# A decode block's backward pass: the chunk load and its staging buffer become a ring of two, and the next chunk is loaded half a chunk ahead

## The chip, the cores and the metric

The kernel runs on one core of one Trainium2 chip. The metric is the device time of one execution in microseconds (us), lower is better. Executions of one kernel in the same rounds mostly lie within half a per cent of their median (the widest set, `ring_slots61`, runs from 1462.4 to 1474.6 us). All runs quoted here are of the fast state. "Faster" is said of a difference of more than 2%.

## The reference, cut to what matters

The program computes one transformer block for a single token (forward) and the gradients of nine inputs (backward). The attention has 32 heads of width 192 over a cache of 8192 positions; K and V have 100 MB each, and their gradients as much again.

```python
def _fwd_reference(A_x, A_k_cache, A_v_cache, A_wq, A_wo, B_x, ..., c, w_mod):
    mod = (_silu(c) @ w_mod).reshape(c.shape[0], 6, 1, -1)     # w_mod: 640 x 3840
    ...
    h = _layernorm(x, axis=-1) * (1 + ca) + sa
    x = x + ga * _A_ref(h, A_k_cache, A_v_cache, A_wq, A_wo)   # wq: 640 x 6144
    h = _layernorm(x, axis=-1) * (1 + cb) + sb
    x = x + gb * _B_ref(h, B_w1, B_w2, B_w3, B_w4)
    return x

def reference(...):
    _out, _vjp = jax.vjp(_f, A_x, A_k_cache, A_v_cache, A_wq, A_wo, B_w3, B_w4, c, w_mod)
    return (_out, *_vjp(grad_out))
```

Two matrices matter here, wq and w_mod. For a matrix W with y = x W the backward pass needs two things: W times the gradient of y (so W is read again), and the outer product of x with the gradient of y (a matrix as large as W, which is written). The kernel does both for 768 columns at a time, a **chunk** of 960 KB: eight chunks of wq, five of w_mod.

## The kernel before

The backward stage is a loop over 64 steps (32 heads, two halves of the cache). Each step loads 1.5 MB of V, computes dP, dS, dV and dK, and stores 3 MB. Between its parts the loop calls `slot()` four times, which runs the next pieces of side work from one list: the wo transposes (`g_do`), dWo (`g_dwo`), and the chunks (`g_chunk`, five pieces for each half of a chunk).

```python
    def load_w(view3, lo, hi):                 # one load buffer ("w", bufs=1)
        w = wst.tile([P, ND, CW], BF16, name="w_st", tag="w", bufs=1)
        nc.sync.dma_start(out=w[:, :, 0 : hi - lo], in_=view3[:, :, lo:hi])
        return w
    # ... (cut)
    def next_w():
        if wseq:
            view, n = wseq.pop(0)
            cur["next"] = load_w(view, n * CW, (n + 1) * CW)
    # ... (cut)
    def g_chunk(b, v3, rows, dst, n, acc, lay):          # half b of chunk n
        lo = n * CW
        if b == 0:
            cur["w"] = cur.pop("next")
            cur["stg"] = bst.tile([P, ND, CW], BF16, name="stg")   # one staging buffer
        w = cur["w"][:, :, b * PW : (b + 1) * PW]
        stg = cur["stg"][:, :, b * PW : (b + 1) * PW]
        # ... (cut) piece 1: cast of the vector
        yield
        wT = bst.tile([P, 15 * P], BF16, name="wT", tag="wT")
        transposed(0, cols, ND, wT)            # piece 2: first use of the loaded chunk (TensorE)
        # ... (cut)
        yield
        transposed(8, cols, ND, wT)            # piece 3: last use of this half
        if b == 1:
            next_w()                           # the load of the next chunk
        # ... (cut)
        yield
        # ... (cut) piece 4: matrix times vector
        for i in range(3):
            V_.tensor_scalar(out=stg[:, i, :], in0=v_bc, scalar1=rows[:, i : i + 1], ...)
        yield
        V_.tensor_tensor(out=acc, in0=ps, in1=acc, op=ALU.add)     # piece 5
        for i in range(3, ND):
            V_.tensor_scalar(out=stg[:, i, :], in0=v_bc, scalar1=rows[:, i : i + 1], ...)
        if b == 1:
            nc.gpsimd.dma_start(out=dst[:, :, lo : lo + CW], in_=cur["stg"])
        yield
    # ... (cut) the order of the side work: after every fourth pair of heads a w_mod chunk
    for t in range(NT):
        # ... (cut)
        jobs.append((5, g_dq(t)))              # half of a wq chunk
        if t % 4 == 3 and late:
            jobs.append((10, g_wm(late.pop(0))))   # a w_mod chunk, at once behind it
    jobs.append((2, g_finish_x()))
    for n in late + list(range(GX)):           # two w_mod chunks, one behind the other
        jobs.append((10, g_wm(n)))
    # ... (cut) the end of a step
        if s + 4 < NS:
            v_l[s + 4] = load_v((s + 4) // 2, s % 2)     # 1536 KB, SyncE's queue
        if s + 2 < NS:
            er_l[s + 2] = load_er(s + 2)                 # 8 KB, SyncE's queue
```

In the timelines below TensorE and SyncE take their instructions in the order of the program text: while TensorE waited 9.18 us for a chunk (until 1013.75 us) it ran nothing else, and while SyncE waited for a store (`ring_first_piece`) the V and er loads behind it waited too. Loads are issued by SyncE, stores by GpSimd. **er** is the 8 KB of (unnormalised) attention weights that TensorE needs for the dV of one step (matmul `dv_ps`); in the views `KB` is a tile (in this stage mostly the output buffers of dV and dK), `stg` the staging buffer, `w_st` the load buffer, DVE is VectorE, POOL is GpSimd, and PEld are TensorE's weight loads.

## Time and profile before

| | kernel before |
|---|---|
| time, median | 1498.7 us |
| profiled span | 1495.2 us |
| moved over the span | 576 MB, 385 GB/s |
| TensorE's waits for chunk loads, from 650 us on | 35.7 us in 4 |

The page's first part has busy time, share of the span and number of instructions of each engine; its last part the transfers (source, issuing queue, count, size).

```profile
PE 1143.8 (77%) x12579; PEld 773.2 (52%) x12579; DVE 1121.6 (75%) x1391; ACT 891.5 (60%) x1966; POOL 106.7 (7%) x190
...
v_sb<-in_A_v_cache_dram SPq DMA_DIRECT2D x128, 1536.0 KB
w_st<-in_A_wq_dram SPq DMA_DIRECT2D x16, 960.0 KB
w_st<-in_w_mod_dram SPq DMA_DIRECT2D x8, 960.0 KB
```

No engine is full over the span, and the chunk loads share SyncE's queue with the V loads. The rows of the page that show the DMA engines as the bound, and the three holes in their rate, stand in the prediction.

### The profile page before, as it was taken

Reading aid. Unit: us, or ns where it says so; the run is one execution under the profiler, and the core shown is the slowest. Engines: PE = TensorE matmul, PEld = TensorE weight load, DVE = VectorE, ACT = ScalarE, POOL = GpSimd, SP = SyncE. Lnnn points to the kernel's source line nnn. Section 1 sums busy time; section 2 is a strip of 40 time slices with the busy share of each in tenths; the row PEclk is TensorE's granted clock in tenths of the full one; section 3 lists DMA queues with packets and bytes.
Section 4 is the critical chain, followed back from the end, with each engine's and each line's share of the span. In section 5 each row is a group of like instructions: output and inputs, shape, how many; then the busy total and the mean of one; then the engine's idle time right before and its main releaser. Section 6 shows DMA issues by size and latency. Waiting matters only on the chain.

```text
span 1495.2 us, 30163 instructions
## 1 busy us (share of the span) xinstructions
PE 1143.8 (77%) x12579; PEld 773.2 (52%) x12579; DVE 1121.6 (75%) x1391; ACT 891.5 (60%) x1966; POOL 106.7 (7%) x190
## 2 busy tenths in 40 slices
PE   3999999999899997777777667766777576676564
PEld 1677777767677776544444434434444343444332
DVE  5999999999999994566767677756676576776465
ACT  1776777776777765655655555545555455555354
POOL 0000000000000000011011011010110110111010
PEclk8999999999999998655656675555565556655555
DMA  9999999999999986499999999998999989999797
GB/s 377 414 407 419 418 410 395 412 398 402 393 406 395 417 318 260 153 406 420 396 423 419 410 422 399 415 396 312 411 411 415 395 314 392 425 420 397 287 416 317
DMA packets 76471, 576.12 MB, mean 385 GB/s; under 512 B 7310, under 2 KB 25054, under 8 KB 35374
## 3 DMA queue, kind: packets, MB, share of 16 engines
q1 hardware_dynamic: 52074, 347.75, 59.0%
q0 software_dynamic: 24240, 226.44, 35.9%
q8 instruction: 98, 1.61, 0.4%
q14 instruction: 39, 0.32, 0.1%
q10 hardware_dynamic: 20, 0.00, 0.0%
HBM read 347.74 MB, written 226.43 MB: 384 GB/s over the span
## 4 chain that ended last, share of the span: by engine, by line
issue 52%; DVE 19%; PE 12%; ACT 9%; POOL 6%; DMA 1%; POOLq 0%; SPq 0%; DVEq 0%; ACTq 0%
DVE prod L275 9%; ACT vs L333 6%; DVE vs L326 4%; DVE prod L280 3%; PE mp L340 3%; PE dot_ps L286 2%; POOL out_dram L938 2%; POOL out_dram L948 2%; DVE S_h L290 2%; PE mp L344 2%; PE q_ps L248 1%; PE op L348 1%; DMA KB<-in_A_k_cache_dram 1%; PE po L378 1%; POOL out_dram L796 1%
## 5 line engine op out<-in xcount | busy, mean ns | idle before, releaser
L707 ACT CAST KB<-dv_ps 128x768 bf16<-128x768 f32 x512 | 377.3, 813 | 167.5 <-PE dv_ps L706 152.9
L695 PE MATMUL dot_ps<-pq,ident_bf 128*128 128x256 bf16 x1536 | 327.9, 398 | 57.9 <-DVE pq L686 57.9
L333 ACT ACTIVATE vs<-v_sb,Ef 128x192 bf16<-128x192 bf16 x896 | 323.4, 443 | 0.0
L706 PE MATMUL dv_ps<-KB,er_b 1*128 1x192 bf16 x2048 | 179.2, 319 | 145.2 <-ACT KB L707 137.0
L695 PEld LDWEIGHTS <-ident_bf 128*128 128x128 bf16 x1536 | 203.4, 136 | 161.3 <-issue 90.0
L711 DVE TENSOR_TENSOR KB<-qs_bc,dS 128x3072 bf16<-128x3072 bf16 x128 | 223.8, 1749 | 37.4 <-DMA out_dram<-KB 37.3
L686 DVE TENSOR_TENSOR pq<-v_sb,KB 128x3072 bf16<-128x3072 bf16 x128 | 223.7, 1748 | 0.0
L275 DVE TENSOR_TENSOR prod<-KB,qs_bc 128x6144 bf16<-128x6144 bf16 x64 | 214.5, 3352 | 10.2 <-DMA KB<-in_A_k_cache_dram 5.5
L340 PE MATMUL mp<-vs,KB 128*128 128x193 bf16 x2048 | 198.5, 250 | 3.6 <-DVE vs L326 3.1
L583 ACT COPY wT<-wT_ps 128x1024 bf16<-128x1024 bf16 x84 | 81.0, 964 | 200.6 <-PE wT_ps L582 197.2
L706 PEld LDWEIGHTS <-er_b 1*128 1x128 bf16 x2048 | 66.0, 103 | 241.8 <-issue 231.9
L340 PEld LDWEIGHTS <-KB 128*128 128x128 bf16 x2048 | 178.1, 99 | 23.5 <-issue 5.8
L286 PE MATMUL dot_ps<-prod,ident_bf 128*128 128x512 bf16 x384 | 97.3, 391 | 46.6 <-DVE prod L280 46.6
L326 DVE TENSOR_TENSOR vs<-v_sb,E 128x1728 bf16<-128x1728 bf16 x128 | 131.9, 1051 | 0.6 <-ACT E L314 0.6
L280 DVE TENSOR_TENSOR prod<-prod 128x3072 bf16<-128x3072 bf16 x64 | 112.1, 1752 | 0.6
L290 DVE TENSOR_REDUCE dP<-dot_ps 128x32 f32<-128x512 f32 x64 | 44.1, 689 | 90.8 <-PE dot_ps L695 90.8
L344 PE MATMUL mp<-vs,KB 128*64 128x193 bf16 x2048 | 110.7, 251 | 0.0
L344 PEld LDWEIGHTS <-KB 128*64 128x64 bf16 x2048 | 82.8, 110 | 21.1 <-issue 21.1
L582 PE MATMUL wT_ps<-ident_bf,w_st 128*128 128x128 bf16 (+1 forms) x470 | 51.7, 293 | 44.0 <-DMA w_st<-in_w_mod_dram 33.5
L286 PEld LDWEIGHTS <-ident_bf 128*128 128x128 bf16 x384 | 36.0, 99 | 89.4 <-issue 60.5
L774 DVE CAST vrow<-bc_t 3x128 bf16<-3x128 f32 x26 | 7.2, 278 | 98.2 <-PE bc_t L772 98.2
L938 POOL DMA_DIRECT2D out_dram<-KB x64 | 36.4, 569 | 589.5 <-ACT KB L707 589.3
(222 smaller groups left out, 953.6 us busy)
## 6 DMA issues: line engine op xcount, KB each, us to landing
v_sb<-in_A_v_cache_dram SPq DMA_DIRECT2D x128, 1536.0 KB
out_dram<-KB POOLq DMA_DIRECT2D x128, 1536.0 KB, 13.1
KB<-in_A_k_cache_dram SPq DMA_DIRECT2D x64, 1536.0 KB
w_st<-in_A_wq_dram SPq DMA_DIRECT2D x16, 960.0 KB
wo_st<-in_A_wo_dram SPq DMA_DIRECT2D x32, 480.0 KB
out_dram<-stg POOLq DMA_DIRECT2D x14, 960.0 KB, 12.6
out_dram<-stg_o POOLq DMA_DIRECT2D x17, 480.0 KB, 13.6
w_st<-in_w_mod_dram SPq DMA_DIRECT2D x8, 960.0 KB
```

Source lines behind the costliest of these rows:

```text
L275: V_.tensor_tensor(out=prod, in0=src, in1=vec[:, None, :].to_broadcast([P, JH, DH]), op=ALU.mult)
L280: V_.tensor_tensor(out=prod[:, :, 0:w], in0=prod[:, :, 0:w], in1=prod[:, :, w : 2 * w], op=ALU.add)
L286: T_.matmul(ps, lhsT=ident_bf, rhs=prod[:, :, k : k + TS], start=(k == 0), stop=(k == w - TS))
L326: V_.tensor_tensor(out=vs[:, 0:n, 0:DH].rearrange("p j (a b) -> p j a b", b=4), in0=v[:, v0 : v0 + n, :].rearrange("p j (a b) -> p j a b", ...
L333: A_.activation(out=vs[:, k, 0:DH], in_=v[:, v0 + k, :], func=ACT.Copy, scale=Ef[:, j0 + k : j0 + k + 1])
L340: T_.matmul(mp[:, 0:MW], lhsT=kb[:, j0 + k, 0:P], rhs=vs[:, k, 0:MW], start=(q == 0 and k == 0), stop=(z and k == JQ - 1), skip_group_chec ...
L344: T_.matmul(mp[p0 : p0 + 64, MO : MO + MW], lhsT=kb[:, j0 + k, P:DH], rhs=vs[:, k, 0:MW], start=False, stop=(z and k >= JQ - 2), skip_grou ...
L686: V_.tensor_tensor(out=pq[:, q], in0=v_l[s][:, q * JQ : (q + 1) * JQ, :], in1=do_bc[:, None, (s // 2) * DH : (s // 2 + 1) * DH].to_broadca ...
L695: T_.matmul(ps[:, q * JQ : (q + 1) * JQ, :], lhsT=ident_bf, rhs=pq[:, q, :, k : k + TS], start=(k == 0), stop=(k == DH - TS), skip_group_c ...
L706: T_.matmul(ps[:, b, k * DH : (k + 1) * DH], lhsT=er[p0 : p0 + 1, 2 * m + k, :], rhs=doh[p0 : p0 + 1, :], start=True, stop=True)
L707: A_.copy(out=dV4[:, 2 * q : 2 * q + 2, m * PW : (m + 1) * PW], in_=ps[:, :, 0:PW])
L711: V_.tensor_tensor(out=dK[:, lo:hi, :].rearrange("p j (a b) -> p j a b", b=4), in0=qh.rearrange("p (a b) -> p a b", b=4)[:, None, :, :].to ...
```

## The change

The intent: with one load buffer the next chunk can't be loaded before the last transpose of the current one. The change lets the gradient overwrite the chunk in place (each half only after its transposes), so that the former staging buffer is free to take the next chunk, and issues that load in piece 5 of the first half instead of piece 3 of the second. No memory is added.

```diff
     def next_w():
         if wseq:
             view, n = wseq.pop(0)
-            cur["next"] = load_w(view, n * CW, (n + 1) * CW)
+            if cur.setdefault("n", 0) % 2 == 0:
+                w = wst.tile([P, ND, CW], BF16, name="w_st", tag="w", bufs=1)
+            else:
+                w = bst.tile([P, ND, CW], BF16, name="stg")
+            cur["n"] += 1
+            nc.sync.dma_start(out=w, in_=view[:, :, n * CW : (n + 1) * CW])
+            cur["next"] = w
 ...
             cur["w"] = cur.pop("next")
-            cur["stg"] = bst.tile([P, ND, CW], BF16, name="stg")
-        w = cur["w"][:, :, b * PW : (b + 1) * PW]
-        stg = cur["stg"][:, :, b * PW : (b + 1) * PW]
+        w = stg = cur["w"][:, :, b * PW : (b + 1) * PW]
 ...
         transposed(8, cols, ND, wT)
-        if b == 1:
-            next_w()
 ...
-        if b == 1:
-            nc.gpsimd.dma_start(out=dst[:, :, lo : lo + CW], in_=cur["stg"])
+        if b == 0:
+            next_w()
+        else:
+            nc.gpsimd.dma_start(out=dst[:, :, lo : lo + CW], in_=cur["w"])
```

## The prediction

> **What bounds the kernel now.** I read the page's slices first. The span has a forward stage (to about 560 us), a short middle, and a backward stage from about 640 us on. The change touches the backward stage only. There the TensorE is busy seven tenths of the time and the DMA engines nearly always:
>
> ```profile
> PE   3999999999899997777777667766777576676564
> DMA  9999999999999986499999999998999989999797
> GB/s 377 414 407 419 418 410 395 412 398 402 393 406 395 417 318 260 153 406 420 396 423 419 410 422 399 415 396 312 411 411 415 395 314 392 425 420 397 287 416 317
> ```
>
> The reader should see that the third row of the backward part is flat at 395 to 425 GB/s, except for slices 28, 33 and 38 (312, 314, 287), and the last one. So the backward stage is bound by data movement, with three holes in it. I then asked for the waits of the backward stage alone (from 650 us), and looked for one that could make such holes:
>
> ```profile
> POOL out_dram L938 <- ACT KB L707: 585.3, 61, 25.9
> DVE vrow L774 <- PE bc_t L772: 98.2, 22, 15.0
> DVE stg L790 <- DMA out_dram<-stg: 6.0, 1, 6.0
> PE wT_ps L582 <- DMA w_st<-in_w_mod_dram: 33.5, 3, 14.9
> PE wT_ps L582 <- DMA w_st<-in_A_wq_dram: 2.2, 1, 2.2
> ```
>
> The columns are total us, times, longest. The big first row is only the store queue waiting for the next result. The fourth row is the one: TensorE stands still three times for the load of a w_mod chunk, 33.5 us in all. The timelines of SyncE (which issues the loads) and of TensorE show how one hole comes about:
>
> ```profile
> 988.91 0.33 SPq L270 DMA_DIRECT2D v_sb<-in_A_v_cache_dram  x1
> 989.34 0.50 SPq L551 DMA_DIRECT2D er_b<-eT_d  x1
> 992.69 0.38 SPq L188 DMA_DIRECT2D w_st<-in_w_mod_dram  x1
> ...
> 1001.83 2.74 PE L695 MATMUL dot_ps<-pq,ident_bf 128*128 128x256 bf16 x12
> 1013.75 1.03 PE L582 MATMUL wT_ps<-ident_bf,w_st 128*128 128x128 bf16 x8 [9.18 <-DMA w_st<-in_w_mod_dram]
> ```
>
> The load is issued at 992.69, its consumer is reached at about 1004.6 (1013.75 less 9.18), its data are there at 1013.75. The lead is 11.9 us, the flight 21.1 us. The other two are alike: issued 1174.96, wanted 1186.7, there 1196.09 (9.39 us waited); issued 1369.28, wanted 1379.3, there 1394.21 (14.92 us waited). TensorE takes its instructions in order, so the main path (dP, dV, dK of each half head) stands too, and about 10 us later the DMA queues have run dry. The engine table by stretch prices this:
>
> ```profile
> 650.00:1010.00 360.00, 257.35 (x2071) 154.90 (x2069) 244.49 (x340) 199.21 (x281) 40.90 (x70) 0.60 1.01 410
> 1010.00:1050.00 40.00, 26.53 (x227) 16.33 (x228) 26.86 (x36) 21.43 (x30) 3.58 (x6) 0.59 0.83 320
> 1050.00:1170.00 120.00, 90.25 (x715) 52.75 (x712) 81.04 (x125) 68.13 (x97) 12.08 (x22) 0.60 1.01 414
> 1170.00:1220.00 50.00, 31.02 (x246) 18.07 (x243) 28.56 (x36) 23.65 (x33) 4.09 (x7) 0.53 0.85 327
> 1220.00:1380.00 160.00, 113.92 (x959) 68.97 (x956) 116.81 (x187) 86.94 (x121) 20.92 (x35) 0.61 1.00 408
> 1380.00:1430.00 50.00, 28.11 (x225) 16.41 (x225) 24.54 (x37) 20.67 (x29) 3.76 (x7) 0.50 0.79 312
> ```
>
> The last two columns are DMA share and GB/s. Undisturbed stretches run at 408 to 414, call it 412; the three disturbed ones at 320, 327 and 312.
>
> **What the Trainium skill says.** "DMA: Bandwidth & Descriptors", section "Where 436 GB/s comes from", puts the fabric ceiling at 435 GB/s; the trace agrees in that no 40th of the span passes 425 here, so the flat parts have little left. The same page, "Issuing engines are not separate DMA queues", says that transfers of all issuing engines interleave on the same 16 DMA engines: this is why a 960 KB load that alone would need 2.4 us at 412 GB/s (my estimate from its size) takes 21 us behind a V load and beside the stores. "Perfetto Trace Analysis", section "Per-engine timelines", says that a hardware-issued DMA's profiled window does not hold its data movement; so I take flights from issue to consumer (21.1 us), not from the 0.38 us of the issue. "Trainium Kernel Development and Optimization", "Best Practices", says to double-buffer so that DMA overlaps compute: the trace shows what one buffer costs, 33.5 us.
>
> **The change, part by part.** The kernel has 13 chunks in this stage (8 of wq, 5 of w_mod), each worked in two halves of five pieces of side work. There are 206 pieces over 236 slots, four slots to a step; steps are 13.3 us apart (stores at 1079.22 and 1172.31 us, seven steps), so a piece comes every 13.3 / (4 x 206/236) = 3.8 us.
>
> Removed: nothing in instructions or bytes. The 130 scalings of 0.31 us stay, as do 13 loads and 13 stores. The load tile and the staging tile are the same two tiles; they now take turns as load and, in place, as output. Memory is equal.
>
> Moved: the load goes from piece 3 of a chunk's second half to piece 5 of its first half. Where a w_mod chunk follows a wq chunk there are, between issue and use, one dWo piece, three do pieces, five dq pieces and two of the new chunk: 11 pieces x 3.8 = 42 us, against a flight of 21 us. So waits one and two (9.2 + 9.4 us) go away. Between the last two w_mod chunks lie only 5 + 2 pieces, 27 us by that pace. In the trace the place is just after the er load of 1353.93, so about 1355, and the use at 1379.3: 24 us, against a flight of 24.9 us before, which then had one more V load (1365.97) ahead of it. So wait three goes from 14.9 us to 0 to 4 us, and a wait that short leaves the DMA queues filled.
>
> Added: the load must wait for the store of the chunk before the current one to land. Stores land after 12.6 us in the median, at most 19.8. That store is issued five pieces (19 us) earlier or more, so SyncE seldom waits, and then for a few us in which the next V load has no free buffer anyway (V loads come 10 to 16 us apart). The in-place writes come two pieces after the transposes that read the same half, so no engine waits for them. The scaling's one wait for the single staging buffer (6.0 us) goes.
>
> Sum, by bytes not moved at 412 GB/s: 40 x (1 - 320/412) = 8.9 us; 50 x (1 - 327/412) = 10.3 us; 50 x (1 - 312/412) = 12.1 us: 31.3 us together. It agrees with the 33.5 us of TensorE waits, since little was made up afterwards. I take off 3 us for what remains of wait three or of new small waits: 28 us gained. 1498.4 - 28 = 1470 us.
>
> **The rivals.** (1) The transfer was hidden anyway: the DMA is the bound and a TensorE wait costs nothing. For: 10 us of each wait pass with queues still at 420 GB/s. Against: the holes afterwards (share 0.83, 0.85, 0.79) are as large as the waits. Time then 1490 to 1498. (2) A new wait takes the old one's place: SyncE takes its loads in order and may stand for a landing store, holding V and er loads back, or the earlier 960 KB delays the small er loads behind it (TensorE waited once 5.95 us for one, at 1251 us). Against: the store is 19 us old by then. It would give back 5 to 15 us: 1475 to 1485. (3) More is won than the holes: earlier loads free SyncE, and steps speed up. Against: the flat parts are at 408 to 414 GB/s, and the whole of 650 to 1460 us at 412 would save only 33 us. Best case about 1462.
>
> **Range and chances.** The middle is 1470, with rival 3's cap below and rival 2 above: 1460 to 1487. A gain of 2% needs 29.4 to 30 us, that is almost all of the 31.3; I give it 0.38. Within 2%: 0.59. Slower by 2%: 0.03, only if in-place use serialises what I think free.
>
> **What would show it.** In the changed profile TensorE's wait for w_mod should fall from 33.5 to under 6 us; each w_mod load should be issued over 22 us before its first transpose; the GB/s row should have no slice near 310 before the last; TensorE's busy time should not change. I am wrong if holes remain with another releaser (er loads, V loads, stores of a chunk), if SyncE shows waits of over 10 us for a chunk's store, or if the holes vanish while the flat level sinks under 405.

## The result

The changed kernel takes 1463.3 us (median of 4 runs, 1461.9 to 1464.2) against 1498.7 us (4 runs, 1495.2 to 1500.4). The ratio is 0.9763, 95% interval 0.9744 to 0.9783: faster. Ratios in this document are those on record, taken from fast runs of the same rounds; they are not quite the ratio of the medians quoted.

The page of the changed kernel, with the rows of busy time, DMA share and rate in 40 slices:

```profile
PE 1142.1 (78%) x12579; PEld 774.0 (53%) x12579; DVE 1121.8 (77%) x1391; ACT 891.4 (61%) x1966; POOL 106.5 (7%) x190
...
DMA  9999999999999998289999999999999999999997
GB/s 375 416 411 419 399 418 409 401 388 411 405 396 395 416 401 308 91 329 415 394 426 425 403 417 422 412 407 409 424 395 422 387 395 428 413 426 394 422 418 328
```

Busy times are those of before within 2 us. The three holes at slices 28, 33 and 38 are gone: from slice 19 to slice 39 nothing is below 387. The engine table by stretch, over the same microseconds as the disturbed stretches of before, has DMA share and GB/s in its last columns (before: 0.83 and 320, 0.85 and 327, 0.79 and 312):

```profile
1010.00:1050.00 40.00, 30.30 (x254) 18.82 (x252) 28.38 (x43) 23.14 (x32) 4.74 (x8) 0.63 1.01 421
1170.00:1220.00 50.00, 38.85 (x305) 23.15 (x305) 34.28 (x46) 29.24 (x41) 6.58 (x11) 0.53 0.99 404
1380.00:1430.00 50.00, 34.26 (x273) 19.39 (x272) 35.49 (x38) 26.80 (x37) 5.68 (x10) 0.60 1.01 418
```

In the waits of TensorE for a transfer from 640 us on, no chunk is left; one row remains, for the small er loads. (The rows have the releaser, total us, times, longest.)

```profile
PE dv_ps L706 <- DMA er_b<-eT_d: 9.2, 4, 4.3
```

The timelines of SyncE and TensorE show the load and the first use of the second w_mod chunk (lead 42.0 us) and of the last one (26.0 us); neither use waits:

```profile
962.48 0.46 SPq L735 DMA_DIRECT2D stg<-in_w_mod_dram  x1
...
1004.44 1.06 PE L582 MATMUL wT_ps<-ident_bf,stg 128*128 128x128 bf16 x8
...
1335.36 0.51 SPq L735 DMA_DIRECT2D w_st<-in_w_mod_dram  x1
...
1361.40 1.03 PE L582 MATMUL wT_ps<-ident_bf,w_st 128*128 128x128 bf16 x8
```

**Where the time came from.** The 64 steps each issue one dV store, so the stores of the two traces can be laid side by side as a clock. The changed kernel is 0.1 us behind at step 28 and 9.3 us ahead at step 29; 8.2 ahead at step 41 and 17.8 at step 42; 17.2 at step 45 and 22.3 at step 46; 19.0 at step 55 and 33.3 at step 56; 34.1 at the last. The four jumps are 9.4, 9.6, 5.1 and 14.3 us. TensorE's waits of before at these places are 9.18, 9.39, 5.95 (for an er load, at 1251 us) and 14.92 us. Between the jumps the two kernels drift by up to some 5 us (the changed one is 4.8 us behind at step 19 and level again at step 21).

### The profile page after: what moved, and what is told of

Its sections match the earlier page's. It is cut to its first block, busy times and chain, and to the rows that moved or that the text cites. A ratio compares the mean times of both kernels' runs of the same rounds, so it can differ in the third digit from the quotient of the medians.

```text
span 1461.0 us, 30156 instructions
## 1 busy us (share of the span) xinstructions
PE 1142.1 (78%) x12579; PEld 774.0 (53%) x12579; DVE 1121.8 (77%) x1391; ACT 891.4 (61%) x1966; POOL 106.5 (7%) x190
## 4 chain that ended last, share of the span: by engine, by line
issue 43%; DVE 22%; PE 16%; ACT 9%; POOL 5%; DMA 5%; SPq 0%; POOLq 0%; DVEq 0%; ACTq 0%
DVE prod L275 9%; ACT vs L333 5%; DVE vs L326 4%; DVE prod L280 3%; PE mp L340 3%; PE dot_ps L695 3%; PE dot_ps L286 2%; POOL out_dram L942 2%; POOL out_dram L952 2%; DVE S_h L290 2%; PE mp L344 2%; DMA out_dram<-stg_o 1%; DVE pq L686 1%; DMA out_dram<-KB 1%; DMA er_b<-eT_d 1%
## 5 line engine op out<-in xcount | busy, mean ns | idle before, releaser
L711 DVE TENSOR_TENSOR KB<-qs_bc,dS 128x3072 bf16<-128x3072 bf16 x128 | 223.8, 1749 | 45.9 <-DMA out_dram<-KB 45.9
L326 DVE TENSOR_TENSOR vs<-v_sb,E 128x1728 bf16<-128x1728 bf16 x128 | 131.9, 1051 | 0.6 <-ACT E L314 0.6
L314 ACT ACTIVATE E<-S_h,negm 128x256 bf16<-128x256 f32 x32 | 16.2, 508 | 91.3 <-DVE negm L459 91.3
L348 PE MATMUL op<-vs,ones_bf 128*32 128x193 bf16 x2048 | 66.5, 250 | 0.0
## 6 DMA issues: line engine op xcount, KB each, us to landing
out_dram<-stg_o POOLq DMA_DIRECT2D x17, 480.0 KB, 13.9
```

What stands on the lines that cost most here:

```text
L326: V_.tensor_tensor(out=vs[:, 0:n, 0:DH].rearrange("p j (a b) -> p j a b", b=4), in0=v[:, v0 : v0 + n, :].rearrange("p j (a b) -> p j a b", ...
L711: V_.tensor_tensor(out=dK[:, lo:hi, :].rearrange("p j (a b) -> p j a b", b=4), in0=qh.rearrange("p (a b) -> p a b", b=4)[:, None, :, :].to ...
```

## The experiments

The **lead** of a load is the time from its issue to the moment its first use is reached, its **flight** the time from its issue until its data are there. The theory after the result: the gain is the longer lead of the chunk load, and each us of wait for a w_mod chunk costs about one us. The rivals: the ring or the in-place output wins by itself; only holes in the DMA rate cost time; the gain is spread over all chunks. Twelve kernels ran. By the rule of 2% `ring_mid_place`, `ring_last_late`, `split_no_ring`, `ring_act_queue` and `ring_slots61` are unclear against the kernel before (their intervals contain 0.98); what they are used for is whether they lie near the changed kernel (0.9763) or near the kernel before.

### The ring without the earlier place

`ring_old_place`: the changed kernel, load at the old place.

```diff
         transposed(8, cols, ND, wT)
+        if b == 1:
+            next_w()
 ...
-        if b == 0:
-            next_w()
-        else:
+        if b == 1:
             nc.gpsimd.dma_start(out=dst[:, :, lo : lo + CW], in_=cur["w"])
```

> The changed kernel's ring of two and in-place output, but the load put back at piece 3 of the chunk's second half. Theory (the gain is the lead of the load over its use): the three w_mod waits of TensorE come back, each 2 to 3 us shorter than in the kernel before because the load now waits for no transpose and SyncE may issue it right after the er load ahead of it (989 instead of 993 us). Waits together some 26 us, time 1463 + 26 = 1489 us (1484 to 1497). Rival (the ring or the in-place output wins by itself, by freeing SyncE and the staging buffer): no w_mod wait worth naming, 1463 us.

Measured: 1497.6 us, ratio to the kernel before 0.999 (0.9977 to 1.0003). The ring alone wins nothing. The waits of TensorE, and the load and use of the second w_mod chunk:

```profile
PE wT_ps L582 <- DMA w_st<-in_w_mod_dram: 24.6, 2, 12.6
PE wT_ps L582 <- DMA stg<-in_w_mod_dram: 11.9, 1, 11.9
...
988.58 0.43 SPq L735 DMA_DIRECT2D stg<-in_w_mod_dram  x1
...
1013.71 1.04 PE L582 MATMUL wT_ps<-ident_bf,stg 128*128 128x128 bf16 x8 [11.87 <-DMA stg<-in_w_mod_dram]
```

One part of the expectation failed: the load was issued 4.1 us earlier than before (988.58 against 992.69) and yet was used at the same time (1013.71 against 1013.75), so the waits did not shorten; they are 36.5 us against 35.7. The flight of a chunk load is no constant: 21.1 us before, 25.1 us here. (In both, SyncE's queue was still moving the V load issued just ahead, at 988.91 and at 987.61 us, until 994 to 996 us.)

### A place in between

`ring_mid_place`: the load in piece 1 of the second half (`if b == 1: next_w()` after the cast of the vector).

> The changed kernel with the load at piece 1 of the second half, two pieces (7.6 us) ahead of the old place and one to two behind the new. Theory of lead against flight: lead 19 to 24 us against a flight of 21 to 25 us, so waits of 0 to 5 us each, together 3 to 8 us: 1466 to 1471 us. Rival (any place ahead of the transposes' end is as good, the load was only blocked by the single buffer): 1463 us, no wait. Rival (DMA bound, a wait below 10 us is absorbed by filled queues): waits are seen but the time stays 1463 us.

Measured: 1466.1 us, ratio 0.9778 (0.9738 to 0.9818). No wait for a chunk at all. The leads are longer than I had counted: 978.42 to 1008.23, 1152.51 to 1180.93 and 1336.66 to 1361.81, so 29.8, 28.4 and 25.2 us, because in the ring SyncE waits for no transpose and issues the load as soon as it has passed the V and er loads ahead of it. The time fell into the expected band without the expected waits; the er waits are 18.0 us here (9.2 in the changed kernel), which may be the reason. Two pieces ahead of the old place are enough.

### One late load

`ring_last_late`: the changed kernel, only the 13th load at the old place.

```diff
+        if b == 1 and cur["n"] == 12 and "next" not in cur:
+            next_w()
 ...
         if b == 0:
-            next_w()
+            if cur["n"] != 12:
+                next_w()
```

> The changed kernel, but only the 13th and last load (the second of the two w_mod chunks at the end) is put back to the old place. Theory (each wait costs its own length): one w_mod wait of 12 to 15 us at about 1360 us comes back, the other two stay away; 1463 + 13 = 1476 us (1473 to 1479), and the main path loses that much at that one step and nowhere else. Rival (DMA bound, only the hole in the DMA rate counts): 8 to 10 us, 1472 us or less. Rival (the gain is spread over all chunks): 1466 us.

Measured: 1473.8 us, ratio to the kernel before 0.9829 (0.9789 to 0.9868), 10.5 us above the changed kernel. The use of the last chunk on TensorE's timeline:

```profile
1372.54 1.03 PE L582 MATMUL wT_ps<-ident_bf,w_st 128*128 128x128 bf16 x8 [9.50 <-DMA w_st<-in_w_mod_dram]
```

By the clock of the dV stores it is 1.4 us behind the changed kernel at step 55 and 11.7 at step 56, and stays there: the one wait of 9.5 us costs 10.3 us, at once and for good. The wait was shorter than the 12 to 15 us expected (the load was issued at 1349.38, 13.7 us before it was wanted), so the total doesn't tell the two theories apart by itself; that the loss equals the wait does speak for the first.

### The lead without the ring

`split_no_ring`: the kernel before, with its staging buffer, but each half of the next chunk is loaded as soon as that half's transposes are issued.

```diff
-    def next_w():
+    def next_w(half=None):
 ...
-            view, n = wseq.pop(0)
-            cur["next"] = load_w(view, n * CW, (n + 1) * CW)
+            view, n = wseq.pop(0) if half != 0 else wseq[0]
+            if "big" not in cur:
+                cur["big"] = wst.tile([P, 2, ND, PW], BF16, name="w_st", tag="w", bufs=1)
+            for b in range(2) if half is None else (half,):
+                lo = n * CW + b * PW
+                nc.sync.dma_start(out=cur["big"][:, b], in_=view[:, :, lo : lo + PW])
 ...
-            cur["w"] = cur.pop("next")
 ...
-        w = cur["w"][:, :, b * PW : (b + 1) * PW]
+        w = cur["big"][:, b]
 ...
-        if b == 1:
-            next_w()
+        next_w(b)
```

> The kernel before, without a ring and with its separate staging buffer, but the load cut into two half loads, each issued as soon as its half's transposes are issued (half 0 at piece 3 of the first half, half 1 at piece 3 of the second). Theory (lead): half 0 leads its use by 9 pieces or more, 34 us, half 1 by as many, so no w_mod wait and 1463 us (1460 to 1468). Rival (in place or two buffers are what wins): waits or SyncE stalls remain, 1490 to 1498 us. Rival (runs of 768 bytes instead of 1536 slow the loads): no waits, but 1470 to 1475 us.

Measured: 1466.2 us, ratio 0.978 (0.9728 to 0.9831), no wait for a chunk; er waits 19.6 us. The interval covers that of the change. So neither the second buffer nor the in-place output is needed; the lead is what wins. (The plain alternative, two load buffers beside the staging buffer, needs another 7.5 KB per partition, 5 x 768 columns of 2 bytes; no run here tried it. That memory is what the in-place output saves.)

### Why a 960 KB load takes over 20 us

`before_act_queue`: the kernel before, only `nc.sync.dma_start` replaced by `nc.scalar.dma_start` for the chunk loads of this stage.

> The kernel before, place, buffers and staging untouched, but the chunk loads of the backward stage are issued from the ACT queue instead of SyncE's, which also carries the V loads. In the run with the ring at the old place the load was issued 3 to 5 us earlier than before and landed no earlier (1013.71 against 1013.75 us), so its flight seems to be time behind the V load ahead of it on the same queue. Theory (queue place): on a queue of its own the load shares the engines but has nothing ahead of it; flight 7 to 12 us against a lead of 10 to 12 us, waits 0 to 2 us each, time 1463 to 1472 us with the load still at the old place. Rival (the flight is the engines' load, whichever the queue): flight 20 us and waits of 9 to 15 us as before, 1498 us. Rival (ACT's sequencer pays for the issues): waits gone but 1475 to 1490 us.

Measured: 1513.3 us, ratio 1.0104 (1.0073 to 1.0134). My theory fell. On a queue of its own the load was no faster: issued 1000.25, there at 1025.06, 24.8 us; the other three w_mod loads that were waited for took 23.0, 25.2 and 24.8 us. The first rival (the engines' load, whichever the queue) came nearest. The waits for chunks grew to 61.6 us in 8, now for wq chunks too (13.1 us). The waits for er went from 7.6 us to none. The transfer view of that flight (1000.3 to 1025.0 us) has packets, MB and share of the engines by queue; q10 is ACT's, q0 the stores', q1 SyncE's:

```profile
q0 software_dynamic: 768, 6.88, 65.8%
q1 hardware_dynamic: 235, 2.31, 24.0%
q10 hardware_dynamic: 656, 0.98, 10.6%
```

The load's 656 packets have 1.5 KB, the stores' 768 packets 9.0 KB. In packets the two queues are near to each other; in bytes they are 1 to 7. The Trainium skill, "DMA: Bandwidth & Descriptors", section "Queues, rings and completion order", says that each DMA engine goes round-robin between its queue rows, a packet at a time. These counts agree: a load of many small packets gets turns, not bytes, and 656 turns beside 9 KB store packets take about as long as 656 x 9.0 KB / 412 GB/s = 14 us plus the 2.4 us of its own bytes (an estimate from the counts above), before any V packet takes a turn. A lead of 12 us could not hide that.

The sums over a flight could agree by chance. Counts over 2 us stretches, read from the same traces by the transfer view, are stricter. Packets by queue:

| run, stretch (us) | stores | SyncE's queue | ACT's queue |
|---|---|---|---|
| before, 998 to 1000 | 73 | 74 (load) | |
| before, 816 to 818 | 13 | 449 (nearly all load) | |
| before_act_queue, 1006 to 1008 | 74 | 0 | 74 (load) |
| before_act_queue, 1012 to 1014 | 45 | 47 (V) | 44 (load) |
| before_act_queue, 1049 to 1051 | 0 | 0 | 350 (load) |
| before_two_queues (next run), 998 to 1000 | 63 | 63 (load) | 62 (load) |

In the stretches where two or three queues have work throughout, each moves the same number of packets within a few; where the stores pause, a load moves five to six times as many. This also says why only three of the five w_mod loads of the kernel before were waited for: the first (issued 812.76, used 828.36) had a lead of 15.6 us, less than the flight of the second, but the stores paused from 816 to 820 us. Turns are not the whole flight: the load of 1000.25 moved no packet in its first 3.5 us, on a queue with nothing ahead of it.

`before_two_queues` puts that to the test: at the old place, two fifths of the rows on SyncE's queue, three fifths on ACT's.

```diff
-            cur["next"] = load_w(view, n * CW, (n + 1) * CW)
+            w = wst.tile([P, ND, CW], BF16, name="w_st", tag="w", bufs=1)
+            nc.sync.dma_start(out=w[:, 0:2], in_=view[:, 0:2, n * CW : (n + 1) * CW])
+            nc.scalar.dma_start(out=w[:, 2:5], in_=view[:, 2:5, n * CW : (n + 1) * CW])
+            cur["next"] = w
```

> The kernel before with each chunk load of the backward stage split over two queues at the old place: two fifths of its rows on SyncE's queue, three fifths on ACT's. In the run with the whole load on ACT's queue its 656 packets of 1.5 KB took 24.8 us (1000.3 to 1025.1), while the store queue moved 768 packets of 9 KB: the queues seem to take turns packet by packet, so the flight is set by the number of the load's packets and not by what stands ahead of it. Theory (turns by packet): the larger part has 384 packets, flight 384/656 x 25 = 15 us, waits of 3 to 5 us each in place of 9 to 15, time 1473 to 1482 us. Rival (flight is set by bytes and by the engines' load): flight stays 21 to 25 us and so do the waits, 1498 to 1513 us. Rival (the SyncE part still stands behind a V load): waits of 8 us, 1490 us.

Measured: 1492.7 us, ratio 0.9964 (0.995 to 0.9977): a small gain, short of the 1473 to 1482 us. TensorE at the second w_mod chunk (both parts issued at 992.3):

```profile
1007.34 0.39 PE L582 MATMUL wT_ps<-ident_bf,w_st 128*128 128x128 bf16 x2 [4.64 <-DMA w_st<-in_w_mod_dram]
1011.43 0.82 PE L582 MATMUL wT_ps<-ident_bf,w_st 128*128 128x128 bf16 x6 [3.69 <-DMA w_st<-in_w_mod_dram]
```

ACT's part was there after 19.1 us (20.1 and 20.5 at the others), not 15. In 992.3 to 1011.4 us the queues moved 538 (stores), 508 (SyncE) and 400 packets (ACT), so turns are still about even, but with three queues a turn of the load comes round more slowly, and ACT's part moved no packet before 996 us: my scaling by packets had shortened that start as well. Turns by packet explain why the flight is long; they did not let me predict its length to better than 5 us. The third rival's numbers (8 us of wait, 1490 us) were the nearest, 7.9 to 10.0 us and 1492.7 us here, but not for its reason: SyncE's part, issued behind a V load, was there first, and ACT's part ended the wait.

### Earlier still

`ring_first_piece`: the load in piece 1 of the first half (`if b == 0: next_w()` after the cast).

> The changed kernel with the load four pieces earlier still, at piece 1 of the chunk's first half, where for chunks that follow one another the store from the same tile has just been issued (it lands after 12 to 19 us). Theory of the changed place: leads are ample already, so nothing is won; SyncE stands for the store for 5 to 15 us at some five of the chunks and holds the V and er loads behind it back, but V is buffered two steps ahead: 1463 to 1470 us, with waits of TensorE for er growing from 9 to 10 to 25 us. Rival (a wait of SyncE is free): 1463 us and no new er waits. Rival (holding V back empties the DMA queues): 1475 us or more.

Measured: 1477.8 us, ratio 0.9867 (0.9839 to 0.9895), 14.5 us worse than the changed kernel. SyncE's own waits, and TensorE's for er:

```profile
SPq L735 <- DMA out_dram<-stg: 46.4, 6, 17.1
SPq L735 <- DMA out_dram<-w_st: 34.5, 5, 17.4
...
PE dv_ps L706 <- DMA er_b<-eT_d: 30.4, 7, 9.6
```

SyncE stands 81 us in 11 for the store that has just left the same tile, and the V and er loads behind it stand too; er waits grow from 9.2 to 30.4 us. The place in the change is late enough for the store to have landed nearly always (there SyncE waits once for it, 9.5 us). So earlier is not better without end. Of the rivals the third (1475 us or more) came nearest; that it was the DMA queues running empty was not looked into.

### What the remaining waits are worth

Three kernels tried to win the er waits and the thin end.

`ring_er_first` issues er ahead of V (the two `if` blocks at the end of a step exchanged).

> The changed kernel with the er load issued ahead of the V load of the same step instead of after it, to see whether the remaining waits of TensorE for er (9.2 us in 4) can be won. Theory (queue place decides the flight): the 8 KB no longer land behind 1536 KB, er waits fall to under 3 us; every us of wait costs a us, so 1455 to 1460 us. Rival: SyncE now stands for er's buffer (TensorE lags VectorE by up to 12 us) ahead of V, V comes late, waits for V appear: 1463 to 1470 us.

Measured: 1463.6 us, ratio 0.9768 (0.9744 to 0.9793), like the change. The er waits fell to 4.6 us, but 8.0 us of chunk waits came, and the waits of VectorE for stores of the tile KB grew from 45.9 to 59.8 us.

`ring_er_act` issues er from ACT's queue (`load_er(s + 2, nc.scalar)`).

> The changed kernel with the er loads of the loop on ACT's queue instead of SyncE's. Theory (er's flight is time behind V and chunk loads of its own queue): its 8 KB land within 5 us, er waits under 2 us in place of 9, 1455 to 1460 us. Rival (ACT waits for TensorE's last use of the buffer and loses as much): 1463 to 1470 us, with ACT idle time for dv_ps at the er issue.

Measured: 1461.9 us (1457.8 to 1464.7), ratio 0.9761 (0.9737 to 0.9785). No er wait is left, and no gain beyond the spread of the runs: 0.9761 against 0.9763 for the change. Waits of VectorE and ACT for landing stores took their place (before the change 37.3 and 4.0 us, with it 45.9 and 4.5):

```profile
DVE KB L711 <- DMA out_dram<-KB: 56.5, 17, 6.4
ACT KB L707 <- DMA out_dram<-KB: 7.5, 4, 3.7
```

`ring_act_queue` issues the changed kernel's chunk loads from ACT's queue.

> The changed kernel with its chunk loads on ACT's queue. With the load on ACT's queue in the kernel before, TensorE's waits for er were gone (0 us), since no load of 1.5 KB packets stood ahead of er on SyncE's queue; here the lead (26 us at the last chunk, 42 us at the others) exceeds the 25 us flight. Theory: no w_mod wait, er waits under 3 us in place of 9, and a us of wait costs about a us: 1455 to 1460 us. Rival (ACT's sequencer stands for the landing store ahead of a load, and the KB copies behind it with it): waits of ACT for a store of 3 to 10 us at some chunks, 1463 to 1475 us. Rival (er waits cost nothing): 1463 us.

Measured: 1465.8 us (1461.0 to 1472.0), ratio 0.9789 (0.9761 to 0.9817): no er wait, 5.0 us of chunk wait at one place, store waits of 71.8 us on VectorE and ACT together. Nothing won.

`ring_slots61` spreads the side work over 61 steps (`SLOTS = 4 * (NS - 3)`).

> The changed kernel with the side work spread over 61 of the 64 steps instead of 59, to see whether the thin end (DMA share 0.76 over the last 30 us, some 7 us empty) can be filled with chunk traffic. Theory (bytes bound): 3 to 5 us won, 1458 to 1460 us. Rival (the end is bound by the engines' chain at 10 us a step, and more side work there lengthens it): 1463 to 1467 us.

Measured: 1465.6 us (1462.4 to 1474.6), ratio 0.9788 (0.9758 to 0.9817). The last slice rose from 328 to 361 GB/s, but er waits grew to 24.0 us: nothing won, and the two effects were not taken apart.

### What bounds the changed kernel

`ring_fewer_stores`: wrong on purpose, without 15 of the 16 dWo stores (that output is then not written; the others agree with the reference).

```diff
+        if t == 0:
+            nc.gpsimd.dma_start(out=dwo_v[t], in_=stg)
-        nc.gpsimd.dma_start(out=dwo_v[t], in_=stg)
```

> Wrong on purpose: the changed kernel without 15 of its 16 stores of dWo (15 x 480 KB = 7.37 MB less), all engine work kept, to see what bounds the backward stage once the w_mod waits are gone. Theory (bytes: the flat stretches run at 408 to 420 GB/s and nothing else can go faster): 7.37 MB / 412 GB/s = 17.9 us less, 1445 us (1443 to 1452). Rival (the in-order chain of the engines is now the bound, the step of some 12.7 us being theirs): 1460 to 1463 us.

Measured: 1451.6 us, ratio to the kernel before 0.9681 (0.9643 to 0.972): 11.7 us under the changed kernel, two thirds of the 17.9 us expected. The rate from 650 to 1410 us fell to 406 GB/s (412 from 650 to 1430 us in the changed kernel). So bytes are a bound of the changed kernel, but not the only one: a third of the time forecast from the bytes did not come. What stood in its place was not traced, and with 4 runs between 1448.6 and 1457.3 us the share itself is rough.

The waits of the profiled runs beside two times, both less that of the changed kernel: the median (1463.3 us) and the span of the profiled run itself (1461.0 us), to which the waits belong.

| kernel | chunk waits, us | er waits, us | median above the changed kernel, us | profiled span above it, us |
|---|---|---|---|---|
| the changed kernel | 0 | 9.2 | 0 | 0 |
| before | 35.7 | 7.6 | +35.4 | +34.2 |
| ring_old_place | 36.5 | 10.0 | +34.4 | +32.5 |
| before_act_queue | 61.6 | 0 | +50.1 | +53.1 |
| before_two_queues | 26.3 | 0.5 | +29.4 | +26.4 |
| ring_last_late | 9.5 | 7.7 | +10.5 | +12.3 |
| ring_mid_place | 0 | 18.0 | +2.8 | +4.1 |
| split_no_ring | 0 | 19.6 | +2.9 | +3.9 |
| ring_first_piece | 0 | 30.4 | +14.5 | +13.9 |
| ring_er_act | 1.2 | 0 | -1.4 | -2.9 |
| ring_er_first | 8.0 | 4.6 | +0.4 | +5.0 |
| ring_act_queue | 5.0 | 0 | +2.5 | +9.2 |
| ring_slots61 | 1.4 | 24.0 | +2.3 | +5.9 |

In the five kernels with more than 9 us of chunk waits, each us of them goes with 0.8 to 1.3 us of time. The small chunk waits of `ring_er_first` and `ring_act_queue` come with other changes in the waits, and their medians and profiled spans disagree by 5 to 7 us; they say nothing about the price. The changed kernel has 9.2 us of er waits itself: the 9 to 10 us more in `ring_mid_place` and `split_no_ring` go with 3 to 4 us, about the spread of runs made in different calls. Why er waits are so much cheaper is open. One thing bears on it: after the longest of them (11.8 us, at 772 us in `ring_mid_place`) the rate fell to 373 and 269 GB/s for 10 us each, a hole of 4.4 us at 412 GB/s; and the 7.5 us by which that kernel was behind the changed one at step 12 had shrunk to 2.3 at step 15. The loss at a w_mod wait was not won back.

## Why the prediction was right

The time was put at 1470 us with 1460 to 1487 as the range; 1463.3 lies in it. On which side of 2% it would fall I had the odds the other way, 0.59 for within 2% and 0.38 for faster; it came out as faster.

**The bound and the three waits**: right. The holes left with the waits, at the steps where the waits were, and the flat rate stayed (412 GB/s from 650 to 1430 us). Two readings were loose: slice 34 of the flat part is at 392, not 395 or more, and the V loads of the kernel before are some 9 to 28 us apart, not 10 to 16.

**The leads**: right. I put 42 us for the chunk behind a wq chunk and 24 to 27 us for the last one; at the three places of the old waits they were 42.0, 40.5 and 26.0. `ring_old_place` (the ring without the lead, no gain) and `split_no_ring` (the lead without the ring, the whole gain) show that the lead is the cause. So my words that the 33.5 us are "what one buffer costs" were wrong: a second buffer at the old place won none of them back.

**The flight as a constant (21 to 25 us)**: not quite. After a start of some 4 us without a packet it is the time of 656 packet turns beside large store packets, and of the V packets that take turns too; issuing 4 us earlier in `ring_old_place` brought the data no earlier, a second queue made it 24.8 us, splitting it over two queues 19 to 20 us. Where the stores paused it was far shorter. My words that the load takes so long "behind a V load and beside the stores" were half right: beside the stores it is; taking it from behind the V load did not help. No harm came of this, since all w_mod leads of the change exceed 25 us: that margin was not planned for the last chunk, where I had allowed 0 to 4 us of wait.

**The sum**: 28 us against 35.4 measured, the term that was mis-sized. I priced the waits by the hole in the DMA rate (31.3 us) and took off 3 us for what might remain. The jumps of the step clock at the three places are 33.3 us, nearly the waits themselves (33.5), and nothing remained of wait three. To this come the wait for an er load at 1251 us (a jump of 5.1 us, partly lost again by drift) and the wq chunk wait of 2.2 us. I had seen both rows and priced neither.

**The rivals**: the first (hidden anyway) is refuted by the result. The second (a new wait takes the place) did not come true for the change (one SyncE wait of 9.5 us for a store, just under the 10 us that I had set as a sign of being wrong; er waits 9.2 against 7.6 us), but it is real: two runs show it, `ring_first_piece` at a cost of 14.5 us, and `ring_er_act` as a won wait that turned into store waits. The third's cap, 33 us from bytes at 412 GB/s, was passed by 2 us in the medians and 1 us in the profiled spans (34.2 us): I had counted to 1460 us only and left out the thin end behind it (35.2 us at 311 GB/s). Its "best case about 1462" is the 33 us taken off the profiled span; off the 1498.4 us that I used for the middle it is 1465 us, and the result lies below that.

**What the profile was to show**: chunk waits under 6 us (0), w_mod leads over 22 us (26.0 to 56.6), no slice near 310 before the last in the backward stage (lowest 387), TensorE's busy time unchanged (1142.1 against 1143.8 us). All held.

## What to carry to other kernels

Where a stage is bound by transfers, look for the waits of an in-order engine that are followed by a hole in the transfer rate, and price them by their own length: here 0.8 to 1.3 us of time for each us of wait. Measure how long a load takes from its issue until its data are there under the traffic of the stage, not by its size, and set its place so that the lead exceeds this; a second buffer at the old place wins nothing. Do not move it so early that the issuing queue must wait for a store, since every load behind it then waits as well.

## What the Trainium skill lacked or had wrong

- "DMA: Bandwidth & Descriptors", "Queues, rings and completion order", has the round-robin by packet but not what follows for a load of short rows: 960 KB in 656 packets of 1.5 KB took 24.8 us on a queue of its own, and a tenth of the engines' time, while the store queue moved 768 packets of 9.0 KB; in 2 us beside the stores 74 packets against 74, in 2 us without stores 350.
- The same page, "Issuing engines are not separate DMA queues", says that issuing from several engines only saves the sequencer's time of issue. Here the choice of queue moved the whole kernel: chunk loads on ACT's queue instead of SyncE's made it 1% slower (ratio 1.0104) and took the waits for the 8 KB er loads from 7.6 us to none; splitting them over both made it 0.4% faster (0.9964).
- "Trainium Kernel Development and Optimization", "Best Practices", says to double-buffer. No page says how far ahead of its use a load must be issued under other traffic, on which all depended here: the ring of two with the load at the old place had a ratio of 0.999, the lead without a ring 0.978.
- No page that I read says what a wait of one in-order engine costs where transfers are the bound: here 0.8 to 1.3 us for each us of wait for a chunk, but only 3 to 4 us for 9 to 10 us more of waits for er.
